# Linear attention and a rational feed-forward layer on one core: reciprocal and Newton product kept in PSUM, low parts of g, q and the weights made on GpSimd

## The chip, the cores and the metric

The kernel runs on one core of a Trainium2 chip. A core has five engines that each work through a queue of their own in order: TensorE (PE) multiplies matrices into PSUM, VectorE (DVE) and ScalarE (ACT) do elementwise work on SBUF and PSUM, GpSimd (POOL) does elementwise work on SBUF, and SyncE (SP) issues most of the transfers here. Engines meet through semaphores. The metric is the device time of one execution in microseconds, lower is better.

## The reference

Two layers follow each other. The first is linear attention without a softmax, normalised by its root mean square; the second is a feed-forward layer whose activation is a quotient of two polynomials.

```python
def _attn_ref(q, k, v, g_norm):                 # (8, 8, 576, 64) each
    kv = np.einsum('bhsd,bhse->bhde', k, v)
    out = np.einsum('bhsd,bhde->bhse', q, kv)
    rms = np.sqrt(np.mean(out * out, axis=-1, keepdims=True) + 1e-06)
    return (out / rms * g_norm).astype(np.float32)

def _moe_ref(x, w_in, w_out, a, b):             # x (4608, 512), w_in (512, 2048)
    h = x @ w_in
    h2 = h * h
    h3 = h2 * h
    P = a[0] + a[1] * h + a[2] * h2 + a[3] * h3
    Q = 1.0 + np.abs(b[0]) * np.abs(h) + np.abs(b[1]) * h2
    g = P / (Q + 1e-06)
    return (g @ w_out).astype(np.float32)
```

Inputs and outputs are float32. The attention's output, with its heads laid side by side, is x.

## The kernel before

The 4608 tokens are cut into nine tiles t of 512 tokens, and the 2048 hidden columns into 16 chunks c of 128. One chunk of one tile is a slot; the kernel works through 9 x 16 = 144 slots. In a slot, `gemm1` multiplies the tile's x with a chunk of w_in into a PSUM bank h (128 x 512), the elementwise steps make g from h, and `gemm2` multiplies g with a chunk of w_out and adds it to four accumulators of one PSUM bank each. gemm2 runs two slots behind (`LAG`), and gemm1 of the next slot is issued in the present one, so TensorE's queue reads: gemm2 of slot i - 2, the attention's part of slot i, gemm1 of slot i + 1.

Float32 products come in two forms. In tile 0 both operands are plain float32. Later each operand is split into a high part, rounded by a ScalarE copy to float32r, and a low part, the rest; a product is then three matmuls (high by low, low by high, high by high). The function `unsplit` says where gemm2 takes the plain form: tile 0, and in tile 1 the chunks from `LATE` = 12. The low parts of g (`ew_d`, L462), of q (`att_kv`, L316) and of the weights (`split_w`, L231) are VectorE subtractions. The table `schedule` gives for each pair of weight chunks the slots in which it is fetched, converted and split (last column).

The elementwise work of a slot stands in four functions. `ew_a` (L421) has ScalarE square h into d, take |b0 h| into q and a3 h + a2, negated, into u; VectorE makes q = |b1| d + q and u = u h. `ew_d` (L454) makes the parts gh and gl of the slot before. `ew_b` (L434) has VectorE go on with u, and ScalarE take Ln and Exp, so that d becomes about 1 / Q. `ew_c` (L441) multiplies q by d, finishes u with a factor d, and makes g = (q - 2) u, one Newton step of the reciprocal. d, q and u are SBUF tiles with two buffers each. Calls of `fill` between these steps put VectorE work of the attention and of the weight conversion at fixed places of the queue: -1 before u's second step, 0 after the product of q and d, 1 before g, 2 after it.

The attention of tile t + 1 is worked during tile t: kv and q parts in chunks 0, 2, 4, 6 (`att_kv`), the outputs in 1, 3, 5, 7 (`att_o`), the mean square in 8 (`att_ms`), its root in 9, the normalisation in 11 to 13 and the split of x in 14. Of PSUM's eight banks four are accumulators, two belong to h, one ("at") to the attention and one ("ms") to the mean square. `finish` works the last chunk of tile 8 in two halves and writes the output.

Of the kernel before, what the change touches and what calls it, by code (L numbers as in the profile page):

```python
# [23 lines left out]
def linear_attention_then_rational_ffn(  # L24
# [189 lines left out]
    def split_w(u):  # L214
        kind, c = u
        i = units.index(u)
        w = ups.pop(u)
# [6 lines left out]
        ACT.copy(wh, w)
# [117 lines left out]
    def att_ms(t, _):  # L342
        rs[t] = ps_at.tile([P, TW], F32, tag="ms", name=f"ms_{t}", bufs=1)
        for p in range(NPAIR):
            PE.matmul(rs[t][p * Q4:(p + 1) * Q4], sel, sqs.pop((t, p)), start=True, stop=True)  # L345
# [76 lines left out]
    def ew_a(t, c, ph, w=TW):  # L422
        nm = f"{t}_{c}"
        d = work.tile([P, w], F32, tag="d", name=f"d_{nm}")
        q = work.tile([P, w], F32, tag="q", name=f"q_{nm}")
# [1 line left out]
        ACT.activation(d, ph, AF.Square)  # L427
        ACT.activation(q, ph, AF.Abs, scale=b0)  # L428
        DVE.scalar_tensor_tensor(q, d, b1abs, q, ALU.mult, ALU.add)  # L429
        ACT.activation(u, ph, AF.Identity, bias=na[:, 2:3], scale=na[:, 3:4])  # L430
        DVE.tensor_tensor(u, u, ph, ALU.mult)  # L431
        pend[t, c] = (d, q, u)

    def ew_b(t, c, ph, fill=lambda k: None):  # L434
        d, q, u = pend[t, c]
# [1 line left out]
        DVE.scalar_tensor_tensor(u, u, na[:, 1:2], ph, ALU.add, ALU.mult)  # L437
        ACT.activation(d, q, AF.Ln, bias=bias[:, 2:3], scale=QSC)  # L438
        ACT.activation(d, d, AF.Exp, bias=bias[:, 3:4], scale=-1.0)  # L439

    def ew_c(t, c, fill=lambda k: None):  # L441
        d, q, u = pend[t, c]
        DVE.scalar_tensor_tensor(q, q, QEPS, d, ALU.add, ALU.mult)  # L443
# [1 line left out]
        DVE.scalar_tensor_tensor(u, u, na[:, 0:1], d, ALU.add, ALU.mult)  # L445
# [5 lines left out]
        DVE.scalar_tensor_tensor(g, q, 2.0, u, ALU.subtract, ALU.mult)  # L451
        fill(2)

    def ew_d(t, c, w=TW):  # L454
        u = pend.pop((t, c))[2]
# [5 lines left out]
        ACT.copy(gh, u)  # L461
        DVE.tensor_tensor(gl, u, f32(gh), ALU.subtract)  # L462
# [211 lines left out]
```

## Time and profile before

| What | Value |
|---|---|
| median of 3 runs | 918.13 us (917.41 to 918.31) |
| span of the profiled execution | 915.9 us |
| VectorE busy in 300 to 400 us, 700 to 800 us | 86.60 us, 89.57 us |
| ScalarE busy in the same stretches | 75.93 us, 77.12 us |
| GpSimd busy after the first 30 us | 0.00 us |
| granted TensorE clock from 30 us on | 1.00, and 0.99 in the last 16 us |

The span runs from the first to the last instruction of the profiled execution; the profile gives no other time for that execution, and what lies around the span is the difference to the runs' time, 2.2 us against the median. PE and ACT are TensorE and ScalarE, L427 is line 427 of the kernel before. In a row of the timeline the columns are start, duration, engine, line, operation, output<-inputs, and in brackets the engine's idle time ahead and what ended it. In a row of groups the last columns are the sum of busy time, the mean of one in ns, and idle time. A TensorE row's end is modelled, so two starts are compared there. The names are the program's, with buffer numbers left out.

### The profile page before, as it was taken

How to read it: one execution, taken by the hardware profiler on the slowest of the kernel's cores; microseconds unless marked ns; L12 is line 12 of the kernel's file. 1: busy time of each engine (PE TensorE's matmuls, PEld its weight loads, DVE VectorE, ACT ScalarE, POOL GpSimd, SP SyncE). 2: the span in 40 equal slices, each digit the busy share in tenths (PEclk: the TensorE clock that was granted, in tenths of full speed). 3: DMA queues.
4: the chain of work that ended last, by engine and by line, in shares of the span. 5: the costliest groups of instructions: out<-in, count | busy, mean ns of one | idle time of the engine just before them, and what ended most of it. 6: DMA issues, size and time to landing. Idle time of an engine off the chain costs nothing.

```text
span 915.9 us, 11648 instructions
## 1 busy us (share of the span) xinstructions
PE 899.0 (98%) x4292; PEld 679.7 (74%) x4292; DVE 800.2 (87%) x1251; ACT 685.3 (75%) x1163; POOL 4.6 (1%) x32
## 2 busy tenths in 40 slices
PE   7999999999999999999999999999999999999998
...
GB/s 314 373 172 226 34 25 41 92 76 48 1 127 70 18 42 103 65 41 47 87 81 41 48 41 126 42 48 29 98 52 48 0 69 13 48 1 46 1 1 46
DMA packets 24992, 65.89 MB, mean 72 GB/s; under 512 B 2856, under 2 KB 3880, under 8 KB 24936
## 3 DMA queue, kind: packets, MB, share of 16 engines
...
## 4 chain that ended last, share of the span: by engine, by line
PE 83%; DVE 11%; ACT 3%; issue 2%; DMA 1%; ACTq 0%; DVEq 0%
PE h L417 13%; PE h L419 12%; PE h L418 12%; PE acc L478 11%; PE acc L479 11%; PE acc L480 11%; PE acc L474 3%; PE h L413 2%; PE kvp L301 2%; DVE q L429 1%; DVE u L445 1%; DVE q L443 1%; PE idle L533 1%; DVE u L437 1%; PE ms L345 1%
## 5 line engine op out<-in xcount | busy, mean ns | idle before, releaser
L427 ACT ACTIVATE d<-h 128x512 f32<-128x512 f32 x143 | 85.7, 599 | 160.6 <-PE h L419 146.9
L417 PE MATMUL h<-x,parts 128*128 128x512 f32 (+1 forms) x516 | 205.8, 399 | 0.0
L419 PE MATMUL h<-x,parts 128*128 128x512 f32 (+1 forms) x516 | 200.5, 389 | 0.0
L479 PE MATMUL acc<-wol,gh 128*128 128x512 f32 x492 | 191.6, 389 | 0.7 <-DVE wol L231 0.7
L429 DVE SCALAR_TENSOR_TENSOR q<-d,b1abs,q 128x512 f32<-128x512 f32 x143 | 107.1, 749 | 81.5 <-ACT q L428 81.2
L418 PE MATMUL h<-x,wil 128*128 128x512 f32 (+1 forms) x452 | 175.5, 388 | 0.0
L478 PE MATMUL acc<-parts,gl 128*128 128x512 f32 x440 | 171.6, 390 | 0.2 <-DVE gl L462 0.2
L480 PE MATMUL acc<-parts,gh 128*128 128x512 f32 x440 | 171.2, 389 | 0.0
L438 ACT ACTIVATE d<-q,bias 128x512 f32<-128x512 f32 x143 | 105.4, 737 | 29.9 <-DVE q L429 28.8
L417 PEld LDWEIGHTS h<-x,parts 128*128 128x128 f32 x516 | 96.9, 188 | 26.4 <-DVE gl L462 5.0
L419 PEld LDWEIGHTS h<-x,parts 128*128 128x128 f32 x516 | 96.9, 188 | 20.6
L430 ACT ACTIVATE u<-h,na 128x512 f32<-128x512 f32 x143 | 112.0, 783 | 0.0
L479 PEld LDWEIGHTS acc<-wol,gh 128*128 128x128 f32 x492 | 92.4, 188 | 20.0 <-DVE wol L231 1.0
L439 ACT ACTIVATE d<-d,bias 128x512 f32<-128x512 f32 x143 | 103.5, 724 | 4.6
L445 DVE SCALAR_TENSOR_TENSOR u<-u,na,d 128x512 f32<-128x512 f32 x143 | 106.5, 745 | 0.0
L437 DVE SCALAR_TENSOR_TENSOR u<-u,na,h 128x512 f32<-128x512 f32 x143 | 106.0, 741 | 0.3
L443 DVE SCALAR_TENSOR_TENSOR q<-q,d 128x512 f32<-128x512 f32 x143 | 98.4, 688 | 1.3 <-ACT d L439 1.3
L431 DVE TENSOR_TENSOR u<-u,h 128x512 f32<-128x512 f32 x143 | 97.8, 684 | 0.9
L428 ACT ACTIVATE q<-h,ab 128x512 f32<-128x512 f32 x143 | 98.1, 686 | 0.0
L418 PEld LDWEIGHTS h<-x,wil 128*128 128x128 f32 x452 | 85.0, 188 | 16.2 <-issue 0.2
L478 PEld LDWEIGHTS acc<-parts,gl 128*128 128x128 f32 x440 | 82.6, 188 | 18.5 <-DVE gl L462 1.1
L480 PEld LDWEIGHTS acc<-parts,gh 128*128 128x128 f32 x440 | 82.6, 188 | 17.1
...
## 6 DMA issues: line engine op xcount, KB each, us to landing
...
```

The costliest lines, as they stand in the source:

```text
L417: PE.matmul(ph, wh, xl, start=(kc == 0), stop=False)
L418: PE.matmul(ph, wl, xh, start=False, stop=False)
L419: PE.matmul(ph, wh, xh, start=False, stop=(kc == NPAIR - 1))
L429: DVE.scalar_tensor_tensor(q, d, b1abs, q, ALU.mult, ALU.add)
L430: ACT.activation(u, ph, AF.Identity, bias=na[:, 2:3], scale=na[:, 3:4])
L437: DVE.scalar_tensor_tensor(u, u, na[:, 1:2], ph, ALU.add, ALU.mult)
L438: ACT.activation(d, q, AF.Ln, bias=bias[:, 2:3], scale=QSC)
L443: DVE.scalar_tensor_tensor(q, q, QEPS, d, ALU.add, ALU.mult)
L445: DVE.scalar_tensor_tensor(u, u, na[:, 0:1], d, ALU.add, ALU.mult)
L478: PE.matmul(o, gl[:, ss], wh, start=(c == 0), stop=False)
L479: PE.matmul(o, gh[:, ss], wl, start=False, stop=False)
L480: PE.matmul(o, gh[:, ss], wh, start=False, stop=(c == NF - 1))
```

## The change

The denominator is factored: q = (|b1 h| + |b0|) h, whose absolute value is |b0||h| + |b1| h h. ScalarE takes v = |b1 h|; VectorE adds |b0| and multiplies by h, which it reads from PSUM; ScalarE takes the absolute value of q from SBUF. The Square is gone. Ln and Exp write their result r into a PSUM bank (`r_bank`, one buffer, in the place of "ms"), and VectorE's product (q + 1 + 1e-6) r is written back into that bank. In `ew_c`, u's step with r now stands ahead of that product, and `fill(0)` ahead of both. The mean square uses the attention's bank. The three kinds of low part are made by GpSimd. `unsplit` is true in tile 0 alone, so the last w_out chunks of tile 1 are split too, and the last two weight pairs are split at slots 28 and 30 in place of 33 and 35.

```diff
-        ("wo", 12): (6, 11, 12, 33),
-        ("wo", 14): (7, 12, 13, 35),
+        ("wo", 12): (6, 11, 12, 28),
+        ("wo", 14): (7, 12, 13, 30),
...
-        return t == 0 or t == 1 and c >= LATE
+        return t == 0
...
-            DVE.tensor_tensor(wl, w, f32(wh), ALU.subtract)
+            POOL.tensor_tensor(wl, w, f32(wh), ALU.subtract)
...
-                DVE.tensor_tensor(ql, q, f32(qh), ALU.subtract)
+                POOL.tensor_tensor(ql, q, f32(qh), ALU.subtract)
...
-        rs[t] = ps_at.tile([P, TW], F32, tag="ms", name=f"ms_{t}", bufs=1)
+        rs[t] = ps_at.tile([P, TW], F32, tag="at", name=f"ms_{t}", bufs=1)
...
-        ACT.activation(d, ph, AF.Square)
-        ACT.activation(q, ph, AF.Abs, scale=b0)
-        DVE.scalar_tensor_tensor(q, d, b1abs, q, ALU.mult, ALU.add)
+        ACT.activation(v, ph, AF.Abs, scale=b1)
+        DVE.scalar_tensor_tensor(q, v, b0abs, ph, ALU.add, ALU.mult)
         ACT.activation(u, ph, AF.Identity, bias=na[:, 2:3], scale=na[:, 3:4])
         DVE.tensor_tensor(u, u, ph, ALU.mult)
...
+        ACT.activation(q, q, AF.Abs)
         DVE.scalar_tensor_tensor(u, u, na[:, 1:2], ph, ALU.add, ALU.mult)
-        ACT.activation(d, q, AF.Ln, bias=bias[:, 2:3], scale=QSC)
-        ACT.activation(d, d, AF.Exp, bias=bias[:, 3:4], scale=-1.0)
+        ACT.activation(r, q, AF.Ln, bias=bias[:, 2:3], scale=QSC)
+        ACT.activation(r, r, AF.Exp, bias=bias[:, 3:4], scale=-1.0)
...
-        DVE.scalar_tensor_tensor(q, q, QEPS, d, ALU.add, ALU.mult)
         fill(0)
-        DVE.scalar_tensor_tensor(u, u, na[:, 0:1], d, ALU.add, ALU.mult)
+        DVE.scalar_tensor_tensor(u, u, na[:, 0:1], r, ALU.add, ALU.mult)
+        DVE.scalar_tensor_tensor(r, q, QEPS, r, ALU.add, ALU.mult)
         fill(1)
...
-        DVE.scalar_tensor_tensor(g, q, 2.0, u, ALU.subtract, ALU.mult)
+        DVE.scalar_tensor_tensor(g, r, 2.0, u, ALU.subtract, ALU.mult)
...
-        DVE.tensor_tensor(gl, u, f32(gh), ALU.subtract)
+        POOL.tensor_tensor(gl, u, f32(gh), ALU.subtract)
...
+    def r_bank(t, c):
+        return ps_at.tile([P, TW], F32, tag="r", name=f"r_{t}_{c}", bufs=1)
```

The built programs show each engine's order, with the semaphores that an instruction waits for (those of the engine that is named; Pool is GpSimd). The first place is ScalarE's queue in tile 2, from chunk 10's first step to its Exp. Before:

```order
L427 ACTIVATE d_2_10_2434<-h_2_10_2416 128x512 [waits PE_49]
L428 ACTIVATE q_2_10_2435<-h_2_10_2416,ab_87 128x512
L430 ACTIVATE u_2_10_2436<-h_2_10_2416,na_93 128x512 [waits DVE_49]
L461 CAST gh_2_9_2442<-u_2_9_2386 128x512 [waits DVE_49]
L438 ACTIVATE d_2_10_2434<-q_2_10_2435,bias_101 128x512 [waits DVE_49]
L439 ACTIVATE d_2_10_2434<-d_2_10_2434,bias_101 128x512 [waits Activation_49]
```

And with the change, at the same place:

```order
L426 ACTIVATE v_2_10_2520<-h_2_10_2502,ab_87 128x512 [waits PE_49]
L428 ACTIVATE u_2_10_2522<-h_2_10_2502,na_93 128x512 [waits DVE_49,Pool_49]
L461 CAST gh_2_9_2527<-u_2_9_2471 128x512
L435 ACTIVATE q_2_10_2521<-q_2_10_2521 128x512
L437 ACTIVATE r_2_10_2531<-q_2_10_2521,bias_101 128x512 [waits Activation_49]
L438 ACTIVATE r_2_10_2531<-r_2_10_2531,bias_101 128x512 [waits Activation_49]
```

Before, the Identity (L430) waited for VectorE's gl of chunk 8, the last reader of its u buffer, and Ln (L438) was the step that waited for this chunk's q. Now the Identity (L428) waits for VectorE's q of this same chunk, which reads the same bank h, and for GpSimd's gl of chunk 8; gh, the new Abs, Ln and Exp stand behind it.

The second place is VectorE's queue for the same chunk, up to the next chunk's q. Before:

```order
L429 SCALAR_TENSOR_TENSOR q_2_10_2435<-d_2_10_2434,b1abs_95,q_2_10_2435 128x512 [waits Activation_49]
L431 TENSOR_TENSOR u_2_10_2436<-u_2_10_2436,h_2_10_2416 128x512 [waits Activation_49]
L462 TENSOR_TENSOR gl_2_9_2443<-u_2_9_2386,gh_2_9_2442 128x512 [waits PE_49,Activation_49]
L437 SCALAR_TENSOR_TENSOR u_2_10_2436<-u_2_10_2436,na_93,h_2_10_2416 128x512 [waits DVE_49]
L443 SCALAR_TENSOR_TENSOR q_2_10_2435<-q_2_10_2435,d_2_10_2434 128x512 [waits Activation_49]
L445 SCALAR_TENSOR_TENSOR u_2_10_2436<-u_2_10_2436,na_93,d_2_10_2434 128x512 [waits DVE_49]
L451 SCALAR_TENSOR_TENSOR u_2_10_2436<-q_2_10_2435,u_2_10_2436 128x512 [waits DVE_49]
L429 SCALAR_TENSOR_TENSOR q_2_11_2489<-d_2_11_2488,b1abs_95,q_2_11_2489 128x512 [waits Activation_49]
```

With the change:

```order
L427 SCALAR_TENSOR_TENSOR q_2_10_2521<-v_2_10_2520,b0abs_95,h_2_10_2502 128x512 [waits Activation_49]
L429 TENSOR_TENSOR u_2_10_2522<-u_2_10_2522,h_2_10_2502 128x512 [waits Activation_49]
L436 SCALAR_TENSOR_TENSOR u_2_10_2522<-u_2_10_2522,na_93,h_2_10_2502 128x512 [waits DVE_49]
L444 SCALAR_TENSOR_TENSOR u_2_10_2522<-u_2_10_2522,na_93,r_2_10_2531 128x512 [waits DVE_49,Activation_49]
L445 SCALAR_TENSOR_TENSOR r_2_10_2531<-q_2_10_2521,r_2_10_2531 128x512
L451 SCALAR_TENSOR_TENSOR u_2_10_2522<-r_2_10_2531,u_2_10_2522 128x512 [waits DVE_49]
L427 SCALAR_TENSOR_TENSOR q_2_11_2576<-v_2_11_2575,b0abs_95,h_2_11_2559 128x512 [waits Activation_49]
```

gl has left this queue; the first row now reads h, and L444, L445 and L451 read r, whose last writer on ScalarE is Exp (L438).

The third place is GpSimd's queue in the first three slots of tile 1, which was empty after the start of the program before. wil and wol are low parts of w_in and w_out, each for two chunks:

```order
L230 TENSOR_TENSOR wil2_1053<-wiw2_294,parts1_1008 128x1024 [waits PE_49,Pool_49]
L462 TENSOR_TENSOR gl_1_0_1063<-u_1_0_998,gh_1_0_1062 128x512 [waits DVE_49,PE_49,Activation_49]
L230 TENSOR_TENSOR wol0_1113<-wow0_326,parts1_1008 128x1024 [waits Activation_49,Pool_49]
L230 TENSOR_TENSOR wil4_1115<-wiw4_373,parts2_1072 128x1024 [waits Activation_49,Pool_49]
L462 TENSOR_TENSOR gl_1_1_1125<-u_1_1_1057,gh_1_1_1124 128x512 [waits DVE_49,PE_49,Activation_49]
L315 TENSOR_TENSOR ql_2_1_1162<-qr_2_1_1030,qh_2_1_1161 128x512 [waits DMAHW6_49,PE_49,Activation_49]
```

The low parts of weights, g and q share this one queue in the order of the program.

More of the change, by code (lines that the diff above doesn't have):

```diff
@@ L76, in linear_attention_then_rational_ffn @@
     POOL.tensor_scalar(na, ab[:, 0:4], -1.0, None, ALU.mult)
-    b1abs = const.tile([P, 1], F32, name="b1abs")
-    b0 = ab[:, 4:5]
+    b0abs = const.tile([P, 1], F32, name="b0abs")
+    b1 = ab[:, 5:6]
     ghalf = const.tile([P, 1], F32, name="ghalf")
@@ L423, in ew_a, with ew_b @@
         nm = f"{t}_{c}"
-        d = work.tile([P, w], F32, tag="d", name=f"d_{nm}")
+        v = work.tile([P, w], F32, tag="d", name=f"v_{nm}")
         q = work.tile([P, w], F32, tag="q", name=f"q_{nm}")
         u = work.tile([P, w], F32, tag="u", name=f"u_{nm}")
-        ACT.activation(d, ph, AF.Square)
-        ACT.activation(q, ph, AF.Abs, scale=b0)
-        DVE.scalar_tensor_tensor(q, d, b1abs, q, ALU.mult, ALU.add)
+        ACT.activation(v, ph, AF.Abs, scale=b1)
+        DVE.scalar_tensor_tensor(q, v, b0abs, ph, ALU.add, ALU.mult)
         ACT.activation(u, ph, AF.Identity, bias=na[:, 2:3], scale=na[:, 3:4])
         DVE.tensor_tensor(u, u, ph, ALU.mult)
-        pend[t, c] = (d, q, u)
-    def ew_b(t, c, ph, fill=lambda k: None):
-        d, q, u = pend[t, c]
+        pend[t, c] = (q, u)
+    def ew_b(t, c, ph, r, fill=lambda k: None):
+        q, u = pend[t, c]
         fill(-1)
+        ACT.activation(q, q, AF.Abs)
         DVE.scalar_tensor_tensor(u, u, na[:, 1:2], ph, ALU.add, ALU.mult)
-        ACT.activation(d, q, AF.Ln, bias=bias[:, 2:3], scale=QSC)
-        ACT.activation(d, d, AF.Exp, bias=bias[:, 3:4], scale=-1.0)
+        ACT.activation(r, q, AF.Ln, bias=bias[:, 2:3], scale=QSC)
+        ACT.activation(r, r, AF.Exp, bias=bias[:, 3:4], scale=-1.0)
+        pend[t, c] = (q, u, r)
     def ew_c(t, c, fill=lambda k: None):
-        d, q, u = pend[t, c]
-        DVE.scalar_tensor_tensor(q, q, QEPS, d, ALU.add, ALU.mult)
+        q, u, r = pend[t, c]
         fill(0)
-        DVE.scalar_tensor_tensor(u, u, na[:, 0:1], d, ALU.add, ALU.mult)
+        DVE.scalar_tensor_tensor(u, u, na[:, 0:1], r, ALU.add, ALU.mult)
+        DVE.scalar_tensor_tensor(r, q, QEPS, r, ALU.add, ALU.mult)
         fill(1)
@@ L499, in finish @@
         (ca, pa), (cb, pb) = parts
+        r = r_bank(t, c)
         ew_a(t, ca, pa, w)
         ew_d(t, c - 1)
-        ew_b(t, ca, pa)
+        ew_b(t, ca, pa, r[:, 0:w])
         gemm2(t, c - 2)
@@ L506, in finish @@
         ew_d(t, ca, w)
-        ew_b(t, cb, pb)
+        ew_b(t, cb, pb, r[:, w:])
         ew_c(t, cb)
@@ L555, in linear_attention_then_rational_ffn @@
     x0 = xpool.tile([P, NPAIR, TW], F32, tag="xB", name="x0")
-    idle = ps_at.tile([P, TW], F32, tag="ms", name="idle", bufs=1)
+    idle = ps_at.tile([P, TW], F32, tag="r", name="idle", bufs=1)
     ctx.enter_context(tc.manual_schedule())
@@ L569, in linear_attention_then_rational_ffn @@
         fetch_w(u)
-    ms0 = ps_at.tile([P, TW], F32, tag="ms", name="ms_0", bufs=1)
+    ms0 = ps_at.tile([P, TW], F32, tag="r", name="ms_0", bufs=1)
     for p in range(NPAIR):
@@ L581, in linear_attention_then_rational_ffn @@
     ACT.copy(x0[:, NPAIR - 1], o0[NPAIR - 1])
-    ACT.activation(b1abs, ab[:, 5:6], AF.Abs)
+    ACT.activation(b0abs, ab[:, 4:5], AF.Abs)
     conv_a(units[2])
     for p in range(NPAIR):
-        pool, tag, bufs = ((ps_h, "h", 2), (ps_h, "h", 2), (ps_at, "at", 1), (ps_at, "ms", 1))[p]
+        pool, tag, bufs = ((ps_h, "h", 2), (ps_h, "h", 2), (ps_at, "at", 1), (ps_at, "r", 1))[p]
         rb = pool.tile([P, TW], F32, tag=tag, name=f"rb_0_{p}", bufs=bufs)
@@ L604, in linear_attention_then_rational_ffn @@
             rest[0].append(lambda u=u: conv_b2(u))
-        ew_b(t, c, ph, lambda k: [f() for f in rest[k]])
+        ew_b(t, c, ph, r_bank(t, c), lambda k: [f() for f in rest[k]])
         for u in at_slot(3, i):
```

3 lines of the change are left out of this document (1 added, 2 removed).

## The prediction

> **What bounds the kernel now.** I read the page first: busy shares, then the chain of work that ended last.
>
> ```profile
> PE 899.0 (98%) x4292; PEld 679.7 (74%) x4292; DVE 800.2 (87%) x1251; ACT 685.3 (75%) x1163; POOL 4.6 (1%) x32
> PE 83%; DVE 11%; ACT 3%; issue 2%; DMA 1%; ACTq 0%; DVEq 0%
> ```
>
> TensorE carries the chain; VectorE's 11% lies in tile 0 and at the end. So for tiles 1 to 8 the question is whether another engine's period per chunk grows beyond TensorE's. The timeline of one plain chunk (tile 8, no attention in it) gives both; columns are start, duration, engine, line.
>
> ```profile
> 870.08 0.60 ACT L427 ACTIVATE d<-h 128x512 f32<-128x512 f32 x1 [1.71 <-PE h L419]
> 870.58 0.68 ACT L428 ACTIVATE q<-h,ab 128x512 f32<-128x512 f32 x1
> 871.15 0.78 ACT L430 ACTIVATE u<-h,na 128x512 f32<-128x512 f32 x1
> 871.81 0.63 ACT L461 CAST gh<-u 128x512 fp32r<-128x512 f32 x1
> 872.32 0.74 ACT L438 ACTIVATE d<-q,bias 128x512 f32<-128x512 f32 x1
> 873.09 0.72 ACT L439 ACTIVATE d<-d,bias 128x512 f32<-128x512 f32 x1
> ...
> 871.29 0.75 DVE L429 SCALAR_TENSOR_TENSOR q<-d,b1abs,q 128x512 f32<-128x512 f32 x1 [0.81 <-ACT q L428]
> 871.96 0.69 DVE L431 TENSOR_TENSOR u<-u,h 128x512 f32<-128x512 f32 x1
> 872.56 0.68 DVE L462 TENSOR_TENSOR gl<-u,gh 128x512 fp32r<-128x512 f32 x1
> 873.17 0.74 DVE L437 SCALAR_TENSOR_TENSOR u<-u,na,h 128x512 f32<-128x512 f32 x1
> 873.85 0.69 DVE L443 SCALAR_TENSOR_TENSOR q<-q,d 128x512 f32<-128x512 f32 x1
> 874.46 0.75 DVE L445 SCALAR_TENSOR_TENSOR u<-u,na,d 128x512 f32<-128x512 f32 x1
> 875.24 0.69 DVE L451 SCALAR_TENSOR_TENSOR u<-q,u 128x512 f32<-128x512 f32 x1
> 876.73 0.75 DVE L429 SCALAR_TENSOR_TENSOR q<-d,b1abs,q 128x512 f32<-128x512 f32 x1 [0.81 <-ACT q L428]
> ```
>
> ```profile
> 872.60 0.39 PE L417 MATMUL h<-x,parts 128*128 128x512 f32 x1
> 875.32 0.39 PE L478 MATMUL acc<-parts,gl 128*128 128x512 f32 x1
> ```
>
> The first product's 12 matmuls take 875.32 - 872.60 = 2.72 us; with the second product's 12 a plain chunk costs TensorE 5.44 us, which is also the distance of the two rows L429 (871.29 to 876.73). VectorE idles 0.81 us in it and ScalarE 1.71: **here TensorE sets the pace with little to spare**. Two step rules are read off. An instruction that waits for another engine or for its predecessor's result starts 0.03 to 0.04 us after that one ends (873.81 to 873.85; 872.32 + 0.74 to 873.09). An independent one overlaps its predecessor by about 0.1: L430 to L461 0.66, L461 to L438 0.51, L443 to L445 0.61.
>
> **The new wait.** Before, L429 reads only SBUF, so L430 (reading h) runs beside it. After, VectorE's q reads h, and the new order makes ScalarE's Identity wait for VectorE (the rows of tile 2, chunk 10). Behind it in ScalarE's queue stand gh, the new Abs, Ln and Exp. VectorE's u, r and g need Exp, and the next chunk's q stands behind g. So q, Identity, gh, Abs, Ln, Exp, u, r, g, next q become one ring: its length is the period, and two chunks of lag before the second product do not shorten it. Before, Identity and gh lay outside: q, Ln, Exp, q, u, g, about 0.78 + 0.77 + 0.76 + 0.61 + 0.78 + 0.60 = 4.3 us, less than 5.44.
>
> For the operations not seen, the nearest rows:
>
> ```profile
> L256 ACT ACTIVATE r<-r 128x512 f32<-128x512 f32 x9 | 5.7, 633 | 0.3
> L254 ACT ACTIVATE r<-ms,bias 128x512 f32<-128x512 f32 x9 | 6.0, 672 | 1.1 <-PE ms L572 1.1
> ```
>
> Abs from SBUF without a pointer scalar: 0.63, as L256 (bounds 0.60 and 0.69, L427 and L428). Ln from PSUM takes 0.67 (L254) where L438 from SBUF takes 0.74, so Exp, now reading PSUM, gets 0.67. Nothing before writes PSUM from ScalarE or VectorE. I take no change, and as bounds what the source changed, 0.065 either way, for Ln, Exp and r each.
>
> Ring, start to start: q 0.75 + 0.03; Identity 0.66; gh 0.51; Abs 0.63 + 0.03; Ln 0.74 + 0.03; Exp 0.67 + 0.04; u 0.66; r 0.69 + 0.03; g 0.60. **Sum 6.07 us** against 5.44, with bounds 5.85 and 6.30. The multiplication u by h and u's second step fall into VectorE's wait for Exp, so the removed gl (0.68) returns nothing.
>
> VectorE's operand place: L431 reads h and takes 0.69, L462 reads SBUF alone and takes 0.68, so I add nothing for PSUM operands. [...]
>
> **What hangs on the ring per tile.** ScalarE has 6.07 - 4.72 = 1.35 us free per period (4.72 is its own cycle v, q, Identity, gh, Abs, Ln, Exp).
>
> ```profile
> L249 DVE TENSOR_TENSOR kvl<-kvp,kvh 64x64 fp32r<-64x64 f32 x56 | 12.2, 218 | 1.5 <-ACT kvh L242 1.1
> L380 DVE SCALAR_TENSOR_TENSOR xf<-xf,ghalf,rb 128x512 f32<-128x512 f32 x28 | 20.3, 744 | 0.0
> L272 DVE TENSOR_TENSOR x<-xf,x 128x512 fp32r<-128x512 f32 x32 | 21.3, 686 | 0.9 <-ACT x L268 0.8
> L486 ACT COPY ob<-acc 128x512 f32<-128x512 f32 x32 | 16.2, 590 | 0.0
> L259 DVE SCALAR_TENSOR_TENSOR r<-ms,r 128x512 f32<-128x512 f32 x9 | 6.2, 689 | 2.0 <-ACT r L256 2.0
> ```
>
> kvl (two between r and g) adds 0.37 in four chunks: 1.5. The norm (L380) stands at the same place: 0.55 three times and 0.66 for the second of chunk 13: 2.3. In chunk 14 the x splits wait for casts behind Exp, and two follow g: 2.9. The rstd's three ScalarE steps and two VectorE ones in chunk 9: 1.4. Four evacuation copies plus sq and xf before the next v: 1.5. Together 9.6, so a full tile takes 16 x 6.07 + 9.6 = **106.7 us**. Before:
>
> ```profile
> 305.70 0.99 PE ms L345 x8
> 400.76 1.00 PE ms L345 x8
> ```
>
> 95.1 us from one tile's ms to the next, 5.9 per chunk on TensorE; the ring's mean with its additions is 6.7.
>
> **Tile 0** has no gh or gl, but weight conversions on VectorE.
>
> ```profile
> L429 DVE SCALAR_TENSOR_TENSOR q<-d,b1abs,q x143: 739/750/754, 35.7 to 898.5; 128x512 f32<-128x512 f32 x143
> 116.05 0.75 DVE L429 SCALAR_TENSOR_TENSOR q<-d,b1abs,q 128x512 f32<-128x512 f32 x1
> 116.71 0.68 DVE L431 TENSOR_TENSOR u<-u,h 128x512 f32<-128x512 f32 x1
> 122.97 0.74 DVE L429 SCALAR_TENSOR_TENSOR q<-d,b1abs,q 128x512 f32<-128x512 f32 x1
> 152.44 0.74 DVE L429 SCALAR_TENSOR_TENSOR q<-d,b1abs,q 128x512 f32<-128x512 f32 x1
> 64.85 3.43 PE h L413 x8
> 96.13 3.45 PE h L413 x8
> ```
>
> VectorE is full there: a chunk is 6.92 us, 116.05 to 122.97. From q to the product with h it took 0.66; now it waits out Identity, 0.75 + 0.03 + 0.78 + 0.03 = 1.59: **0.93 more per chunk**. The later conversions now stand ahead of the wait for Exp and hide it. Fourteen chunks give 13.0; from 64.85 to 96.13 TensorE already set 7.8 us per chunk, which takes off some 1.8. Chunks 14 and 15 become latency-bound (9.4 + 5.6 against 12.85): 2.1. Tile 0 was 152.44 - 35.7 = 116.7 and becomes 130.0. The first q comes 0.5 earlier, without the Square.
>
> **Tile 1** also splits weights.
>
> ```profile
> L224 ACT CAST parts<-wiw 128x1024 fp32r<-128x1024 f32 x8 | 8.3, 1039 | 0.0
> 238.65 3.43 PE acc L474 x8
> L85 POOL MEMSET kvf<- 128x1024 f32 x1 | 1.0, 951 | 0.0
> ```
>
> A cast L224 adds 0.94 to ScalarE's cycle. In its first nine chunks ScalarE has 12 of them, the q, kvh, sq and xf copies (0.95 per chunk) and one evacuation: 4.72 plus these, never under the ring, sums to 64.4. The other seven take 50.0 (ring, norms, rstd, splits, the last cast). Together 114.4.
>
> The late w_out chunks go from 3.43 us (L474, four fp32 products) to 2.72: 4 x 0.71 = 2.8 us less on TensorE, worth nothing under a longer ring. gl, ql and the weights' low parts move to GpSimd, which has nothing else to do. No row shows its two-input operation: bounds are the write-only 0.95 for 1024 columns (L85) and three times VectorE's 0.68, 2.05, for gl. gl is needed two chunks later, when its u is overwritten and the product reads it, 6 us of cover; cost taken: nothing. Moving ms into the attention bank costs nothing either: its neighbours there are a chunk away.
>
> **Sum.** First q 35.2; tile 0 130.0; tile 1 114.4; tiles 2 to 6 533.5; tile 7, without kvl, 105.2; tile 8's 15 chunks 15 x 6.07 + 0.6 = 91.6. The tail:
>
> ```profile
> 903.05 0.48 DVE L429 SCALAR_TENSOR_TENSOR q_15.0_7669<-d_15.0_7668,b1abs,q_15.0_7669 128x256 f32<-128x256 f32 x1
> 909.42 0.43 DVE L462 TENSOR_TENSOR gl_15.5_7717<-u_15.5_7700,gh_15.5_7716 128x256 fp32r<-128x256 f32 x1 [0.53 <-ACT gh_15.5_7716 L461]
> ```
>
> From the first half's q to the last gl's end it took 6.8; two half rings and GpSimd's gl (0.85, between VectorE's 0.43 and three times that) make 9.6, so the 12.9 us to the end become 15.7. Total 1025.6, against the profiled span of 915.9, which lies 2.2 under the median of the runs (918.13). With 2.2 around it: **1028 us**.
>
> **Rivals.** (1) PSUM shortens the ring: if each of the six operations on r gains 0.1, the ring is 5.5. A tile is then 16 x 5.5 + 9.6 = 97.6 against 95.1, and the time about 955. For it: L254 against L438, but that is 0.065. [...]
>
> (2) TensorE keeps the pace, and it gets **faster**: that needs VectorE's instructions with one SBUF operand to be quicker than those with two. It decides at 0.16 us each: the ring's four lose 0.64 and it fits into 5.44, and tile 0's six lose the 0.93. Then the 2.8 us of the late w_out chunks count: 918.1 - 2.8 = 915. For it stands the 98%; against it, again, L431 and L462, alike within 0.01.
>
> (3) GpSimd becomes a bound: at three times VectorE's time, 12 weight parts (3.7 each) and nine gl and five ql (2.05) fill 73 us of the 64 in tile 1's start, and the last gl comes 1.2 later: about 1028 + 9 + 1 = 1038. [...]
>
> (4) GpSimd takes its share and nothing else happens, since VectorE's idle time is not the bound: that is contained in my forecast.
>
> **Chances.** Forecast 0.80, (1) 0.09, (2) 0.04, (3) 0.07. The ring's bounds are -0.22 and +0.23 over 127 chunks, -28 and +29 us, which holds (3) too; 10 us more are given towards (1): 990 to 1060. A measurement tells 0.2% from no change. Faster is (2) less a near miss, 0.03; same 0.01; slower 0.96.
>
> **What would show it.** ScalarE's Identity with idle time ended by VectorE's q in every chunk, about 0.8 us; VectorE idle before its step with r, ended by Exp, 1.3 us; q rows 6.1 apart in tile 8; TensorE's busy share down, waiting for VectorE; ms rows 107 apart. Rows q 5.44 apart would prove me wrong; an Exp or Ln under 0.6 would show rival (1), TensorE waiting for GpSimd's gl rival (3).

## The result, and the profile after

The changed kernel takes **1035.49 us** (median of 4 runs, 1035.01 to 1035.68) against 917.9 for the kernel before on the same chip: a ratio of 1.1281, 95% interval 1.1266 to 1.1296. It is slower by 117.6 us; forecast were 1028, in a range of 990 to 1060.

The page of the changed kernel: busy time, the chain that ended last, and four groups (sum of busy time, mean in ns, idle time ahead and what ended it).

```profile
PE 936.4 (91%) x4308; PEld 684.4 (66%) x4308; DVE 717.8 (69%) x1082; ACT 698.3 (68%) x1167; POOL 244.3 (24%) x205
ACT 39%; DVE 39%; PE 15%; issue 4%; DMA 2%; POOL 1%; ACTq 0%; DVEq 0%; POOLq 0%
L428 ACT ACTIVATE u<-h,na 128x512 f32<-128x512 f32 x143 | 111.3, 778 | 283.2 <-DVE q L427 283.2
L462 POOL TENSOR_TENSOR gl<-u,gh 128x512 fp32r<-128x512 f32 x127 | 163.5, 1287 | 568.3 <-ACT gh L461 553.5
L444 DVE SCALAR_TENSOR_TENSOR u<-u,na,r 128x512 f32<-128x512 f32 x143 | 106.7, 746 | 118.6 <-ACT r L438 118.6
L429 DVE TENSOR_TENSOR u<-u,h 128x512 f32<-128x512 f32 x143 | 98.3, 687 | 128.8 <-ACT u L428 128.8
```

VectorE has lost 82 us of work (800.2 to 717.8) and the kernel is slower: no engine is busy throughout now. TensorE's share of the chain fell from 83% to 15%, and ScalarE and VectorE carry it in equal parts, which fits a ring between the two. In all 143 chunks ScalarE's Identity (L428) waits for VectorE's q (L427), and VectorE's product with h (L429) waits for that Identity; in 121 of them its step with r (L444) waits for Exp (L438).

One plain chunk of tile 8 in the timeline of the changed kernel, ScalarE and then VectorE, to be laid beside the prediction's chunk of before:

```profile
989.04 0.78 ACT L428 ACTIVATE u<-h,na 128x512 f32<-128x512 f32 x1 [2.25 <-DVE q L427]
989.72 0.61 ACT L461 CAST gh<-u 128x512 fp32r<-128x512 f32 x1
990.23 0.63 ACT L435 ACTIVATE q<-q 128x512 f32<-128x512 f32 x1
990.89 0.69 ACT L437 ACTIVATE r<-q,bias 128x512 f32<-128x512 f32 x1
991.62 0.66 ACT L438 ACTIVATE r<-r,bias 128x512 f32<-128x512 f32 x1
...
988.21 0.73 DVE L427 SCALAR_TENSOR_TENSOR q<-v,b0abs,h 128x512 f32<-128x512 f32 x1
989.85 0.69 DVE L429 TENSOR_TENSOR u<-u,h 128x512 f32<-128x512 f32 x1 [0.91 <-ACT u L428]
992.31 0.75 DVE L444 SCALAR_TENSOR_TENSOR u<-u,na,r 128x512 f32<-128x512 f32 x1 [0.99 <-ACT r L438]
992.98 0.69 DVE L445 SCALAR_TENSOR_TENSOR r<-q,r 128x512 f32<-128x512 f32 x1
993.70 0.69 DVE L451 SCALAR_TENSOR_TENSOR u<-r,u 128x512 f32<-128x512 f32 x1
994.31 0.74 DVE L427 SCALAR_TENSOR_TENSOR q<-v,b0abs,h 128x512 f32<-128x512 f32 x1
```

Follow the starts: q 988.21, Identity 989.04, gh 989.72, Abs 990.23, Ln 990.89, Exp 991.62, u 992.31, r 992.98, g 993.70, next q 994.31. Each begins within 0.1 us of the end of the one ahead, and the whole is **6.10 us**, where the chunk before was 5.44. ScalarE isn't short of time in it: it idles 2.25 us ahead of the Identity.

The table sets the q rows against the prediction's terms: when the first q starts, how far a tile's first q lies from the next tile's, and from the last q to the end (us, from the trace of each kernel's profiled execution; e1, e4, e6, e11 and e12 are experiments below).

| | forecast | after | before | e1 | e4 | e6 | e11 | e12 |
|---|---|---|---|---|---|---|---|---|
| first q | 35.2 | 34.7 | 35.7 | 35.2 | 34.8 | 34.7 | 35.0 | 35.3 |
| tile 0 | 130.0 | 131.7 | 116.7 | 121.2 | 117.3 | 118.4 | 120.6 | 120.6 |
| tile 1 | 114.4 | 119.2 | 99.8 | 104.4 | 113.6 | 104.2 | 99.9 | 107.2 |
| tile 2 | 106.7 | 107.0 | 97.6 | 95.9 | 93.5 | 95.2 | 98.0 | 97.0 |
| tiles 3 to 6, mean | 106.7 | 107.1 | 95.6 | 96.2 | 95.6 | 95.6 | 96.2 | 96.9 |
| tile 7 | 105.2 | 105.5 | 91.0 | 92.1 | 91.0 | 91.0 | 92.2 | 92.6 |
| tile 8, 15 chunks | 91.6 | 92.1 | 79.9 | 80.3 | 80.1 | 79.9 | 80.3 | 80.1 |
| tail | 15.7 | 15.2 | 12.9 | 13.7 | 13.1 | 12.9 | 13.6 | 13.7 |

The largest shortfall is tile 1's, 4.8 us, and then tile 0's, 1.7. Most of it lies in three pairs of rows; here are two of them and one that behaves otherwise (VectorE, then the GpSimd instruction that runs at that time).

```profile
154.90 2.43 DVE L271 TENSOR_TENSOR x<-xf,x 128x512 fp32r<-128x512 f32 x1 [1.94 <-ACT x L267]
154.43 2.35 POOL L230 TENSOR_TENSOR parts<-wiw,parts 128x1024 fp32r<-128x1024 f32 x1 [139.64 <-ACT parts L223]
...
257.19 2.75 DVE L379 SCALAR_TENSOR_TENSOR xf<-xf,ghalf,rb 128x512 f32<-128x512 f32 x1
257.00 2.40 POOL L230 TENSOR_TENSOR wol<-wow,parts 128x1024 fp32r<-128x1024 f32 x1 [1.63 <-ACT parts L223]
...
254.19 0.75 DVE L436 SCALAR_TENSOR_TENSOR u<-u,na,h 128x512 f32<-128x512 f32 x1
254.07 1.29 POOL L462 TENSOR_TENSOR gl<-u,gh 128x512 fp32r<-128x512 f32 x1 [5.33 <-ACT gh L461]
```

A VectorE instruction with two inputs in SBUF that starts while GpSimd's 2.4-us subtraction of weights runs takes 2.43 or 2.75 us where it took 0.69 or 0.74: it ends 0.55 and 0.54 us after GpSimd does (157.33 against 156.78; 259.94 against 259.40). A VectorE instruction with one input in SBUF and the other in PSUM (u and h) beside gl keeps its 0.75; of the 143 rows of L436, 124 of which start while GpSimd works on a subtraction, the longest takes 0.78. The third pair stands at 273.48 (2.45). Together they add 1.74 + 2.01 + 1.76 = 5.5 us, one of them in tile 0 and two in tile 1. The delay reaches the period: chunk 12 of tile 1, which holds the second pair, takes 8.64 us from q to q, and chunk 12 of tile 2 takes 6.62.

### The profile page after: what moved, and what is told of

It is laid out like the page before. It is cut to its first block, busy times and chain, and to the rows that moved or that the text cites. A ratio compares the mean times of both kernels' runs of the same rounds, so it can differ in the third digit from the quotient of the medians.

```text
span 1033.9 us, 12124 instructions
## 1 busy us (share of the span) xinstructions
PE 936.4 (91%) x4308; PEld 684.4 (66%) x4308; DVE 717.8 (69%) x1082; ACT 698.3 (68%) x1167; POOL 244.3 (24%) x205
## 4 chain that ended last, share of the span: by engine, by line
ACT 39%; DVE 39%; PE 15%; issue 4%; DMA 2%; POOL 1%; ACTq 0%; DVEq 0%; POOLq 0%
ACT u L428 9%; DVE q L427 8%; ACT r L437 7%; ACT r L438 7%; DVE r L445 6%; DVE u L451 6%; DVE u L444 6%; ACT q L435 5%; ACT gh L461 5%; DVE xf L379 2%; PE h L416 2%; DVE x L271 2%; PE acc L481 2%; PE acc L483 2%; PE acc L482 2%
## 5 line engine op out<-in xcount | busy, mean ns | idle before, releaser
L428 ACT ACTIVATE u<-h,na 128x512 f32<-128x512 f32 x143 | 111.3, 778 | 283.2 <-DVE q L427 283.2
L462 POOL TENSOR_TENSOR gl<-u,gh 128x512 fp32r<-128x512 f32 x127 | 163.5, 1287 | 568.3 <-ACT gh L461 553.5
L481 PE MATMUL acc<-parts,gl 128*128 128x512 f32 x448 | 183.0, 408 | 47.5 <-POOL gl L462 42.1
L482 PE MATMUL acc<-wol,gh 128*128 128x512 f32 x508 | 202.3, 398 | 0.5 <-POOL wol L230 0.5
L444 DVE SCALAR_TENSOR_TENSOR u<-u,na,r 128x512 f32<-128x512 f32 x143 | 106.7, 746 | 118.6 <-ACT r L438 118.6
L429 DVE TENSOR_TENSOR u<-u,h 128x512 f32<-128x512 f32 x143 | 98.3, 687 | 128.8 <-ACT u L428 128.8
L483 PE MATMUL acc<-parts,gh 128*128 128x512 f32 x448 | 176.2, 393 | 0.0
L427 DVE SCALAR_TENSOR_TENSOR q<-v,b0abs,h 128x512 f32<-128x512 f32 x143 | 105.6, 738 | 17.6 <-ACT v L426 17.4
L436 DVE SCALAR_TENSOR_TENSOR u<-u,na,h 128x512 f32<-128x512 f32 x143 | 106.8, 747 | 4.6
L426 ACT ACTIVATE v<-h,ab 128x512 f32<-128x512 f32 x143 | 99.1, 693 | 14.0 <-PE h L418 8.5
L437 ACT ACTIVATE r<-q,bias 128x512 f32<-128x512 f32 x143 | 99.0, 692 | 4.7
L438 ACT ACTIVATE r<-r,bias 128x512 f32<-128x512 f32 (+1 forms) x145 | 95.6, 659 | 4.7
L445 DVE SCALAR_TENSOR_TENSOR r<-q,r 128x512 f32<-128x512 f32 x143 | 98.4, 688 | 0.0
```

Of the source, the lines that this page charges most:

```text
L427: DVE.scalar_tensor_tensor(q, v, b0abs, ph, ALU.add, ALU.mult)
L437: ACT.activation(r, q, AF.Ln, bias=bias[:, 2:3], scale=QSC)
L438: ACT.activation(r, r, AF.Exp, bias=bias[:, 3:4], scale=-1.0)
L444: DVE.scalar_tensor_tensor(u, u, na[:, 0:1], r, ALU.add, ALU.mult)
L462: POOL.tensor_tensor(gl, u, f32(gh), ALU.subtract)
L481: PE.matmul(o, gl[:, ss], wh, start=(c == 0), stop=False)
```

## The experiments

The theory under test: a ring of ScalarE and VectorE steps sets the chunk, because the Identity now waits for q. The rivals: GpSimd's low parts, or what VectorE and ScalarE have to do in sum. No kernel here leaves out any part of the computation.

### e1: the Identity ahead of q

```diff
+        ACT.activation(u, ph, AF.Identity, bias=na[:, 2:3], scale=na[:, 3:4])
         ACT.activation(v, ph, AF.Abs, scale=b1)
         DVE.scalar_tensor_tensor(q, v, b0abs, ph, ALU.add, ALU.mult)
-        ACT.activation(u, ph, AF.Identity, bias=na[:, 2:3], scale=na[:, 3:4])
```

> The changed kernel with the two lines of ScalarE in ew_a exchanged: Identity (u) first, then Abs (v). VectorE's q is then ordered behind both readers of h, and nothing of ScalarE waits for VectorE's q before the new Abs. Theory (ring through the Identity's wait): the ring shrinks from 6.10 to about 4.85 us (q 0.75 + 0.03, Abs 0.63 + 0.03, Ln 0.69 + 0.03, Exp 0.66 + 0.04, u 0.66, r 0.72, g 0.61), under TensorE's 5.44, so q rows in tile 8 stand 5.44 apart again, ms rows about 95 apart, and the time is 905 to 920 us. Rival (GpSimd's low parts, or their blocking of VectorE, cost the time): all of them are still there, so the time stays above 1000 us. Rival (operations on PSUM are slow): they are still there too, 1000 us or more.

Measured: 929.31 us (927.51 to 930.56), ratio 1.0113 (1.0094 to 1.0133), above the 905 to 920 that were expected. One moved line gives back 106 of the 117.6 us. A plain chunk in the timeline of e1, ScalarE and then VectorE:

```profile
885.57 0.78 ACT L426 ACTIVATE u<-h,na 128x512 f32<-128x512 f32 x1 [1.22 <-PE h L418]
886.25 0.68 ACT L427 ACTIVATE v<-h,ab 128x512 f32<-128x512 f32 x1
...
891.01 0.78 ACT L426 ACTIVATE u<-h,na 128x512 f32<-128x512 f32 x1 [1.21 <-PE h L418]
...
886.96 0.75 DVE L428 SCALAR_TENSOR_TENSOR q<-v,b0abs,h 128x512 f32<-128x512 f32 x1 [0.49 <-ACT v L427]
```

Now the Identity waits for TensorE, and the chunk is 5.44 us again (885.57 to 891.01). ScalarE's two reads of bank h stand together ahead of VectorE's, and the ring is cut. It stays 10 us above the kernel before; e6 to e8, e11 and e12 ask where.

### e2: gh out of the ring

In the loop over slots, gh and gl of the slot before are made after Exp, not ahead of Abs:

```diff
-        if i:
-            ew_d(*slots[i - 1])
         ew_b(...)
+        if i:
+            ew_d(*slots[i - 1])
```

> The changed kernel with gh of the chunk before (and its gl) issued behind Exp in place of ahead of the new Abs, tiles 0 to 8 except the last chunk. Theory (ring): gh's 0.51 us leave the ring, 6.10 becomes 5.59; q rows in tile 8 are 5.6 apart; about 118 chunks lose 0.51 us each, so the time is 965 to 985 us. Rivals (GpSimd, PSUM operands): no amount of work changes, gl comes even later, so the time stays at 1035 us or rises.

Measured: 1059.64 us (1057.56 to 1061.61), ratio 1.1533 (1.1506 to 1.1560): a miss of the wrong sign. The ring did lose gh; another took its place. Rows of tile 8 of e2, of GpSimd, TensorE (that waited), ScalarE and VectorE:

```profile
1003.00 1.28 POOL L462 TENSOR_TENSOR gl<-u,gh 128x512 fp32r<-128x512 f32 x1 [5.14 <-ACT gh L461]
...
1004.33 0.50 PE L481 MATMUL acc<-parts,gl 128*128 128x512 f32 x1 [0.69 <-POOL gl L462]
...
1010.11 0.69 ACT L426 ACTIVATE v<-h,ab 128x512 f32<-128x512 f32 x1 [1.60 <-PE h L418]
...
998.78 0.75 DVE L427 SCALAR_TENSOR_TENSOR q<-v,b0abs,h 128x512 f32<-128x512 f32 x1 [0.75 <-ACT v L426]
...
1004.41 0.75 DVE L427 SCALAR_TENSOR_TENSOR q<-v,b0abs,h 128x512 f32<-128x512 f32 x1
...
1010.83 0.75 DVE L427 SCALAR_TENSOR_TENSOR q<-v,b0abs,h 128x512 f32<-128x512 f32 x1 [0.75 <-ACT v L426]
```

TensorE starts the second product as gl lands (1003.00 + 1.28 to 1004.33), then the first product for a later chunk follows (1004.33 + 5.44 = 1009.77), and v waits for that until 1010.11. gh, gl, second product, first product, v, q and on to the next gh but one is a ring over two chunks: the q rows stand 5.63 and 6.42 apart, 6.03 in the mean, a little less than the 6.10 of the changed kernel.

What makes e2 slower than the changed kernel is chunk 0 of tiles 2 to 8: it takes 7.8 to 10.1 us where it took 6.1 to 6.6, in sum 18.7 of the 21.8 us between the two spans. In tile 3 of e2 TensorE waits there for gl, and then for a while its granted clock is at half. The second row is of a stretch: its length, busy time of TensorE, its weight loads, VectorE, ScalarE and GpSimd, then the granted clock and two figures of the DMAs.

```profile
392.42 0.79 PE L481 MATMUL acc<-woh,gl 128*128 128x512 f32 x1 [3.87 <-POOL gl L462]
...
391.40:398.20 6.80, 5.78 (x18) 4.16 (x20) 4.55 (x7) 3.85 (x7) 2.49 (x3) 0.50 0.00 0
```

The 12 products that begin at 392.42 take 5.4 us there where they take 2.72 elsewhere, and TensorE is now a member of the ring. So gl had no 6 us of cover. The changed kernel shows how much it had, GpSimd and TensorE of the plain chunk above:

```profile
990.46 1.28 POOL L462 TENSOR_TENSOR gl<-u,gh 128x512 fp32r<-128x512 f32 x1 [4.81 <-ACT gh L461]
...
991.80 0.50 PE L481 MATMUL acc<-parts,gl 128*128 128x512 f32 x1 [0.34 <-POOL gl L462]
```

Even there TensorE waits for gl, inside the 0.66 us that the longer ring leaves it. In e2 v starts 5.78 us after the second product does (1004.33 to 1010.11). By that lag the v that needs the next first product could start at 991.80 + 5.78 = 997.58, and it starts at 992.20 + 6.10 = 998.30: some 0.7 us are spare, and e2 makes gh 2.0 us later against its Identity (1002.26 against 999.62, in the changed kernel 0.68 behind it).

### e3: all low parts back on VectorE

```diff
-            POOL.tensor_tensor(wl, w, f32(wh), ALU.subtract)
+            DVE.tensor_tensor(wl, w, f32(wh), ALU.subtract)
...
-        POOL.tensor_tensor(gl, u, f32(gh), ALU.subtract)
+        DVE.tensor_tensor(gl, u, f32(gh), ALU.subtract)
```

(ql likewise.)

> The changed kernel with all three low parts (g, q, weights) back on VectorE. Theory (ring): gl falls into VectorE's wait for Exp and costs nothing, ql (0.6 us, 28 times) and the weights' parts (1.14 us, 15 times, partly hidden behind ScalarE) lengthen the ring, the three long VectorE instructions beside GpSimd (5.5 us) go away: 1035 to 1065 us, q rows in tile 8 still 6.1 apart. Rival (GpSimd costs the time): back to 915 to 940 us.

Measured: 1053.41 us, ratio 1.1465 (1.1448 to 1.1483). Without GpSimd the loss is larger, not smaller: GpSimd isn't its cause, and its help is worth 18 us here. The wait of the ring stands as in the changed kernel; in the waits of e3 (total, times, longest):

```profile
ACT u L428 <- DVE q L427: 309.8, 143, 5.9
```

A plain chunk is 6.04 us here, 0.06 less than in the changed kernel. VectorE's q and ScalarE's Identity in e3:

```profile
1011.88 0.74 DVE L427 SCALAR_TENSOR_TENSOR q<-v,b0abs,h 128x512 f32<-128x512 f32 x1
...
1012.65 0.78 ACT L428 ACTIVATE u<-h,na 128x512 f32<-128x512 f32 x1 [2.19 <-DVE q L427]
```

The Identity starts 0.04 us after q's end here, where it waits for VectorE alone. In the changed kernel it is 0.10 (988.94 to 989.04) wherever the Identity waits for GpSimd's gl as well, and 0.04 in tile 0 behind its first chunk, where it doesn't. So the second wait itself lengthens the ring by 0.06 us.

### e4: the kernel before with GpSimd's low parts and the late split

The edits to `split_w`, `att_kv`, `ew_d`, `schedule` and `unsplit` alone, on the kernel before.

> The kernel before with the low parts of g, q and weights on GpSimd and the late w_out chunks split, without the new denominator and the PSUM tile. Theory (ring): no new wait, TensorE keeps the pace at 5.44 us per chunk; 2.8 us come off in tile 1 and the stalls on low parts around 165 us may go: 908 to 918 us, a few us more if VectorE's instructions with two SBUF inputs (it has four of them per chunk here) run into GpSimd's. Rival (GpSimd costs the time): over 1000 us.

Measured: 929.22 us, ratio 1.0115 (1.0097 to 1.0133), slower than expected. By the table tile 1 takes 13.8 us more (4.4 of them come with the late split alone, as e6 shows), tile 2 4.1 less, and the others are as before. Two rows of tile 1 in e4, VectorE and GpSimd:

```profile
163.42 2.73 DVE L450 SCALAR_TENSOR_TENSOR u<-q,u 128x512 f32<-128x512 f32 x1
...
163.09 2.52 POOL L230 TENSOR_TENSOR wol<-wow,parts 128x1024 fp32r<-128x1024 f32 x1 [1.44 <-ACT parts L223]
```

With q and d in SBUF, g's step (L450) and q's step (L428) have two SBUF inputs and are held up beside GpSimd: 2.73 us for 0.69 in the row above, and 2.89 for 0.75 at 173.79, beside a weight part that runs from 173.28 to 176.13. In the changed kernel r and h are in PSUM, and the same steps aren't: the longest of its 143 rows of q (L427) takes 0.75 and of its 143 rows of g's step (L451) 0.69. So the parts of the change aren't independent: the low parts on GpSimd cost some 9 us here over e6, and were worth 18 (e3) and 9.6 (e12) where VectorE's steps read r and h from PSUM.

### e5: r back in SBUF

```diff
-        return ps_at.tile([P, TW], F32, tag="r", name=f"r_{t}_{c}", bufs=1)
+        return work.tile([P, TW], F32, tag="rsb", name=f"r_{t}_{c}", bufs=1)
```

(With the work pool's two buffers.)

> The changed kernel with r in an SBUF tile of two buffers in place of the PSUM bank; everything else as changed. Theory (ring, plus blocking: a VectorE instruction with two SBUF inputs that meets a running GpSimd subtraction waits it out): Ln and Exp take 0.74 and 0.72 again in place of 0.69 and 0.66, so the ring is 6.2 and q rows in tile 8 stand 6.2 apart (+14 us); gl (0.04 us behind gh) ends before u's step with r begins, so tile 8 shows no long VectorE rows; ql and the weights' parts run beside r and g, which now have two SBUF inputs, so the chunks with ql and tile 1 get VectorE rows of 1.5 us and more: 1060 to 1110 us in all. Without blocking: 1045 to 1055 us. Rival (r in PSUM is what costs): back under 1000 us.

Measured: 1099.04 us (1097.92 to 1099.27), ratio 1.1967 (1.1950 to 1.1983); q rows of tile 8 stand 6.32 apart. The groups of Ln, Exp and r's product, in the changed kernel and then in e5:

```profile
L437 ACT ACTIVATE r<-q,bias 128x512 f32<-128x512 f32 x143 | 99.0, 692 | 4.7
L438 ACT ACTIVATE r<-r,bias 128x512 f32<-128x512 f32 (+1 forms) x145 | 95.6, 659 | 4.7
L445 DVE SCALAR_TENSOR_TENSOR r<-q,r 128x512 f32<-128x512 f32 x143 | 98.4, 688 | 0.0
```

```profile
L445 DVE SCALAR_TENSOR_TENSOR r<-q,r 128x512 f32<-128x512 f32 x143 | 122.4, 856 | 4.9
L438 ACT ACTIVATE r<-r,bias 128x512 f32<-128x512 f32 (+1 forms) x145 | 104.4, 720 | 4.7
L437 ACT ACTIVATE r<-q,bias 128x512 f32<-128x512 f32 x143 | 103.4, 723 | 4.7
```

Ln is 0.03 and Exp 0.06 us longer with r in SBUF, and in tile 8 r's product starts 0.78 after u's step, as that ends, not 0.67. The 0.22 us per chunk are 31 us over 143 chunks, half of the 64 between the two kernels. In the chunks where ql is made the q rows stand 7.78 apart (6.46 in the changed kernel), with r's product up to 1.67 us long: both its tensors are now in SBUF beside GpSimd, which fits the blocking. PSUM as r's home helps this kernel; it doesn't cause its loss.

### e6: the late split alone

The kernel before, with the edits to `schedule` and `unsplit` only.

> The kernel before with only the last w_out chunks of tile 1 split and their weight pairs split at slots 28 and 30. TensorE keeps the pace there, so 16 products of 0.86 us become 0.68: 2.8 us less, 914 to 918 us where the kernel before takes 918 to 919. If TensorE were not the bound in tile 1: no difference.

Measured: 920.11 us (11 runs, 918.79 to 921.11), ratio 1.0019 (1.0009 to 1.0028): no gain. Tile 1 takes 4.4 us more and tile 2 2.4 less, since the weight parts come five slots earlier, into chunks 12 and 14 of tile 1, the second of which also splits x (9.66 us from q to q, before 6.75). Tile 0, whose work the edit leaves alone, took 1.7 more in this execution. All of it lies in chunks 4 to 7, where the granted TensorE clock was 0.51 from 63.5 to 67.0 us; in the kernel before it was 1.00 in that stretch. What sets this off isn't shown: just ahead of it TensorE waited 1.95 us for kvl, in both.

### e7 and e8: fewer low parts on GpSimd, on top of e1

e7 leaves VectorE the weight parts that stand at the borders of tiles 0 and 1; e8 leaves GpSimd nothing but gl.

```diff
-            POOL.tensor_tensor(wl, w, f32(wh), ALU.subtract)
+            (DVE if i in (0, NU - 2, NU - 1) else POOL).tensor_tensor(wl, w, f32(wh), ALU.subtract)
```

> Identity first (as e1), and the weights' low parts of three pairs, those made beside the x splits and a norm (slots 14, 28, 30), back on VectorE. Blocking theory: the three VectorE rows of 2.4 to 2.8 us become 0.7, three instructions of 1.2 are added: 3 to 5 us less than e1 (929.3): 923 to 927 us. Without blocking: 2 to 4 us more than e1.

> Identity first (as e1), but GpSimd makes only gl (the two halves of the last chunk on VectorE); ql and the weights' low parts are VectorE's again. No wait on VectorE's q in ScalarE's queue, no long GpSimd instruction: TensorE keeps the pace from tile 1 on, tile 1 gains 2.8 us from the late chunks and about as much from VectorE's missing gl: 910 to 920 us. If gl alone blocks VectorE: 925 us or more.

Measured: e7 929.38 us, ratio 1.0127 (1.0110 to 1.0144), the same as e1; e8 938.23, ratio 1.0218 (1.0204 to 1.0232). Both miss. In e7 chunk 14 of tile 0 gains 0.6 (10.36 to 9.74), but chunk 15 (4.84 to 5.49) and chunk 0 of tile 1 (6.04 to 7.72) lose more. ScalarE waits for TensorE there, and TensorE has half its clock (e7, ScalarE's Identity of tile 1's chunk 0, then the stretch):

```profile
154.98 0.78 ACT L426 ACTIVATE u<-h,na 128x512 f32<-128x512 f32 x1 [1.27 <-PE h L418]
...
149.20:156.00 6.80, 6.09 (x13) 4.47 (x14) 5.82 (x9) 3.01 (x5) 0.00 (x0) 0.50 0.00 0
```

e11 has the same weight part on VectorE at this place, and a clock of 1.00 from 149 to 156 us; these chunks take 4.87 and 6.05 there. So the loss in e7 isn't VectorE's, and as e7's trace is of the longest of its four runs (932.40 us), it doesn't decide what the three blocked instructions cost. In e8 the clock is at 0.50 in the same place (149.3 to 156.1), but most of its loss is VectorE's: all of tile 1 takes 111.7 us from first q to first q where e1 has 104.4, and chunks 2 and 4, in which VectorE makes ql and weight parts again, take 7.63 and 7.62 for 6.06 and 6.05.

### e9 and e10: the Identity twice

A second, equal Identity right behind the first: in e9 in the changed kernel, in e10 in e1.

```diff
         ACT.activation(u, ph, AF.Identity, bias=na[:, 2:3], scale=na[:, 3:4])
+        ACT.activation(u, ph, AF.Identity, bias=na[:, 2:3], scale=na[:, 3:4])
```

> The changed kernel with the Identity of h issued twice, one after the other, ahead of v = h + na. Ring theory: the second one lies in the ring, which grows by one Identity and its gap (0.78 + 0.03 us) from 6.10 to about 6.9 us; tile 8's q stand 6.9 us apart, and 143 chunks times 0.81 us give 116 us more: 1140 to 1155 us. Rival (the chunk is set by the sum of ScalarE's or VectorE's own work, or by TensorE): ScalarE has about 1.3 us idle in each 6.1-us chunk and takes the second Identity into it, within 20 us of 1035.

> The kernel of e1 (Identity of h ahead of v's Abs) with the Identity issued twice. Ring theory: there the Identity isn't in the ring, so a second one costs only what ScalarE's own cycle then exceeds TensorE's: 4.72 + 0.81 = 5.5 us against 5.44, so tile 8's q stand about 5.5 to 5.6 us apart and the time is 930 to 955 us. Rival (an Identity costs its length wherever it stands): 116 us over 929, about 1045.

Measured: e9 1155.19 us (1153.93 to 1155.83), ratio 1.2586 (1.2567 to 1.2605); e10 959.00, ratio 1.0448 (1.0433 to 1.0462). ScalarE's rows of a plain chunk of e9, and behind them of e10:

```profile
1095.04 0.78 ACT L428 ACTIVATE u<-h,na 128x512 f32<-128x512 f32 x1 [2.26 <-DVE q L427]
1095.85 0.78 ACT L429 ACTIVATE u<-h,na 128x512 f32<-128x512 f32 x1
...
1101.95 0.78 ACT L428 ACTIVATE u<-h,na 128x512 f32<-128x512 f32 x1 [2.25 <-DVE q L427]
```

```profile
909.80 0.78 ACT L427 ACTIVATE u<-h,na 128x512 f32<-128x512 f32 x1
...
915.25 0.78 ACT L427 ACTIVATE u<-h,na 128x512 f32<-128x512 f32 x1
```

In e9 the chunk is 6.91 us, 6.10 + 0.81, although ScalarE still idles 2.26 us in it: in this ring the second Identity costs its whole length, however idle its engine. 143 times 0.81 is 116, and 119.7 were measured. In e10 the same instruction costs 29.7 us, and nothing in a plain chunk (5.45): it is paid in the chunks with attention or weight work, 8.9 us in tile 1 (113.3 for 104.4), where ScalarE also has the weights' casts, and 2 to 4 us in each of the other tiles up to 7. ScalarE has time left in some of these chunks, and why those pay too isn't shown. Both times lie above what was expected, by 0.2 and 4 us.

### e11 and e12: what is left of e1

e11 is e1 with the last w_out chunks unsplit as before, and with the weight parts of e7 and the last chunk's halves of gl on VectorE. e12 is e11 with every low part on VectorE.

```diff
-        return t == 0
+        return t == 0 or t == 1 and c >= 12
...
-        POOL.tensor_tensor(gl, u, f32(gh), ALU.subtract)
+        (POOL if w == TW else DVE).tensor_tensor(gl, u, f32(gh), ALU.subtract)
```

> The kernel of e1 with the last w_out chunks unsplit as before the change, and with the weight parts of the first and the last two units and the halves of g's low part on VectorE. If the 11 us that e1 stands above the kernel before come from the borders of tiles 0 to 2 (late split, GpSimd's long subtractions): 914 to 925 us. If they come from GpSimd's subtractions in every chunk: as e1, 927 to 932.

> The kernel of e11 (Identity first, late w_out unsplit) with all low parts back on VectorE, so that against the kernel before only r's product in PSUM, the other Newton form and the new order in the chunk are left. If e11's remaining 8.5 us are GpSimd's: 918 to 921 us. If they are the new form's and order's own (tile 0, where GpSimd makes almost nothing, stands 3.9 us above before in e11; chunks 13 to 15 of every tile 1.4): 925 to 929. If VectorE, with 0.68 us more per chunk, no longer hides r and the next q within 5.44 us: 930 to 940, with TensorE waiting for VectorE.

Measured: e11 926.22 us (925.20 to 928.20), ratio 1.0094 (1.0080 to 1.0107), just above the first case; e12 935.77 (934.45 to 936.12), ratio 1.0187 (1.0172 to 1.0201). e12's time is that of its third case, though not as it was put: a plain chunk keeps its 5.44 us, and the loss lies in tile 1 (107.2 against e11's 99.9), where VectorE splits weights too. With the ring cut, GpSimd's low parts are thus worth 9.6 us.

e11 stands 8.4 us above before by span (924.3 against 915.9): 3.9 in tile 0, 0.6 in each of tiles 3 to 6, 1.2 in tile 7, the rest in small pieces. Of tile 0's 3.9, 1.9 lie in chunks 4 to 7, where the granted clock was 0.50 from 63.3 to 66.7 us, as in e6, and 1.8 in chunks 14 and 15. e12, without GpSimd, has the same tile 0 and the same chunks 13 to 15, so GpSimd isn't what is left. One piece can be read off; rows of chunk 14 of tile 3 in e11, ScalarE and then VectorE:

```profile
439.41 2.18 ACT L267 CAST x<-xf 128x512 fp32r<-128x512 f32 x4
...
440.05 0.69 DVE L271 TENSOR_TENSOR x<-xf,x 128x512 fp32r<-128x512 f32 x1 [1.28 <-ACT x L267]
440.66 0.74 DVE L444 SCALAR_TENSOR_TENSOR u<-u,na,r 128x512 f32<-128x512 f32 x1
```

The change calls `fill(0)` ahead of u's step, so the split of x, which waits for a cast that stands behind Exp, holds up the step with r by 1.1 us (Exp ends at 439.5); before, it stood behind the product of q and d. `fill(0)` back behind a step wasn't tried. No version found beats the kernel before; of those with the new denominator e11 comes nearest.

## Why the prediction was right, point by point

- **The ring: right, and shown.** Foretold 6.07 us from the rows of before, measured 6.10, with every step in the order that was written down: q 0.83 (foretold 0.78; the Identity starts 0.10 after q's end, 0.06 of it for the second wait that e3 lacks), Identity 0.68 (0.66), gh 0.51, Abs 0.66, Ln 0.73 (0.77), Exp 0.69 (0.71), u 0.67 (0.66), r 0.72, g 0.61 (0.60). e1 removes the wait and 106 us with it; e9 lengthens it by 0.81 and pays 119.7 us, e10 pays 29.7 for the same work outside.
- **The per-tile additions: right.** 9.6 us over 16 rings were foretold; tiles 2 to 6 sum to 535.5 against 533.5.
- **Tiles 0 and 1: mis-sized by 1.7 and 4.8 us.** The terms gave GpSimd's work no effect on VectorE. The three blocked instructions account for 1.7 and 3.8 of it; 1 us in tile 1 isn't explained, 0.8 of it in the first nine chunks (65.2 us for the 64.4 of the sum).
- **"6 us of cover" for gl: wrong.** It is about 0.7 us, by the trace and by e2, which used it up. In the changed kernel the cost was still nothing, so the sum didn't notice.
- **2.8 us for the late w_out chunks "under" TensorE's pace: wrong.** e6 gives none: chunk 14 of tile 1, not TensorE, pays for the earlier parts. Rival (2)'s 915 was 2.8 too low on that count.
- **PSUM operands on VectorE cost nothing: right.** q with h from PSUM has a median of 0.736 us, q from SBUF before 0.750; the product with r in PSUM (L445) has a mean of 0.688, that with d in SBUF before (L443) 0.688.
- **PSUM as ScalarE's destination: rival (1) had its sign right and its size wrong.** Ln into PSUM takes 0.692 where 0.74 were entered, Exp the 0.66 foretold as 0.67; VectorE's three operations on r gained nothing. That is 0.06 of the 0.57 us which the rival needed.
- **GpSimd as a bound, rival (3): not so.** gl takes 1.29 us, 1.9 times VectorE's 0.68, where three times, the prediction's upper bound, was its author's estimate. The sign that it named for this rival did show: TensorE waits for gl 60 times, 61.0 us in sum. But the waits fit into the time that the longer ring leaves TensorE, and e3 is slower without GpSimd.
- **The sum.** 1025.6 became 1033.9: first q and tail -1.0, tiles 0 and 1 +6.5, tiles 2 to 8 +2.8. Around the span lie 1.6 us, not 2.2.
